# One transposing DMA per group of blocks for O and per two pairs for k in a windowed-attention and MLP kernel

## The chip, the cores and the metric

The kernel runs on one core of a Trainium2 chip. Its engines are TensorE (PE: matmuls, and PEld: the loads of their stationary operand), VectorE (DVE), ScalarE (ACT), GpSimd (POOL) and SyncE (SP). The metric is device time of one execution in microseconds (us), lower is better. A profile describes one execution; its span runs from the first to the last instruction.

## The reference

Eight batches of eight heads, 576 tokens, head size 64. Attention looks back 64 tokens; its output goes through a two-layer MLP with SiLU between.

```python
scores = scale * np.matmul(q, k.transpose(0, 1, 3, 2))
rel = pos[:, None] - pos[None, :]
mask = (rel >= 0) & (rel < window)            # window = 64
...
attn = np.exp(scores)
attn = attn / (np.sum(attn, axis=-1, keepdims=True) + 1e-09)
out = np.matmul(attn, v)
...
x = attn_out.transpose(0, 2, 1, 3).reshape(B * S, H * D)    # 4608 x 512
h = x @ w_in                                                # 512 x 2048
g = h * (1.0 / (1.0 + np.exp(-h)))
return g @ w_out                                            # 2048 x 512
```

## The kernel before

**Tiling.** The heads of a batch form four pairs (NP), and its 576 tokens nine blocks of 64, taken in three groups (NG) of three blocks. A unit of attention is one pair in one group, so a batch has twelve units, in the order of groups and in each group of pairs. The MLP runs over nine tiles of 512 tokens: sixteen first-layer rows of four accumulating matmuls each (L403), a SiLU on ScalarE into a buffer g (L409), then four second-layer rows of sixteen matmuls (L412), a copy into ot (L418) and a store (L422).

**One unit.** TensorE makes the scores of three blocks from kt and qbd (L317) into a bank of PSUM, ScalarE takes exp (L335), VectorE multiplies with the mask (L338), TensorE multiplies with V (L343), VectorE takes the reciprocal of the row sums (L349) and normalizes. The first layer needs the result with features on the partitions, in the tile bridge.

**Two ways to transpose.** In batches 0 to 2 the result O is turned by TensorE (L383, L394) and copied to bridge (L399). From batch 3 on (NXO) the norm writes rows into ox (L367; two units share one tile, in the upper and the lower half of its partitions), and SyncE issues a transposing DMA per unit, from 64 x 384 to three 128 x 64 pieces of bridge (L388). k of batches 0 and 1 is loaded, cast and turned by TensorE (L282, lifted by L295). From batch 2 on (NXK) GpSimd loads k with a casting DMA per head into kb (L240), and SyncE issues a transposing DMA per pair, from 96 x 768 into kt (L246). q is always loaded in float32 (L228, from batch 3 on by SyncE), cast (L271), turned by TensorE (L282) and lifted into qbd (L289). V goes by GpSimd's DMA (L252). kt, qbd and vv have two buffers each, for even and odd batches.

**Order.** Every engine has its instructions in a fixed order, which a planner (class Plan) works out when the kernel is built. It simulates the engines with given durations. Work is added in classes; each class is a queue of its own, taken strictly in the order of adding, and an engine that comes free takes the head with the lowest rank among the classes whose head has all that it needs. Both kinds of transposes stand in the class "xbar" (L457 and L526, rank -1.5), reckoned with 0.5 us of SyncE each, and 1.45 us (k) or 0.55 us (O) of DMA. The work of a batch is added as: q and k, V, the MLP tiles that have become possible, then attention. GpSimd's loads all stand in the class "dma". q and k of a batch are held back until V of the batch before has landed (L456, L470). Scores are planned only at certain points of the MLP (scores_may_run). At run time each instruction waits for the real events of what it needs, so an instruction that the planner put too early blocks what stands behind it on its engine. This holds for SyncE's queue as well, which has all q loads from batch 3 on, all transposes and all stores.

**Buffers.** kb has four tiles, one for a pair (a batch in all); ox six tiles with twelve units in batches 3 to 7, and one unit per tile in batch 0; g has NFT + 4 = 20 tiles. bridge is four tiles, one for each 128 features, of all 4608 tokens.

Of the kernel before, what the change touches and what calls it, by code (L numbers as in the profile page):

```python
# [9 lines left out]
BF16 = mybir.dt.bfloat16  # L10
# [98 lines left out]
def kernel(ctx, tc, q, k, v, w_in, w_out, out):  # L109
    nc = tc.nc  # L110
    B, H, S, D = q.shape
    d_model, d_ff = w_in.shape
    assert (B, H, S, D) == (8, 8, 576, 64) and (d_model, d_ff) == (512, 2048)
    NP = H // 2
    NB = S // 64
    NM = 6
    NR = S // NM
    NG = 3
    NDC = d_model // 128
    NFT = d_ff // 128  # L120
    TT = 512
    NTT = B * S // TT
    TB = TT // 64
    NK = 2
    NN, NNB, NE, NOB, NOT, NGT = 8, 8, 14, 6, 4, NFT + 4
    PARTS = {0: [(0, 192), (192, 384), (384, TT)], 1: [(0, 256), (256, TT)]}
    NXK, NXO = 2, 3
    NKB, NOX = 4, 6
    scale = 1.0 / float(D) ** 0.5


# [2 lines left out]
    keep = ctx.enter_context(tc.tile_pool(name="keep", bufs=1))  # L134
# [11 lines left out]
    kt = [keep.tile([128, 64 + NP * S], BF16, name=f"kt{i}") for i in range(NK)]  # L146
    vv = [keep.tile([128, H * NB + 1, D + 2], BF16, name=f"vv{i}") for i in range(NK)]
    es = [keep.tile([128, 3, 2, 64], BF16, name=f"e{i}") for i in range(NE)]
    rcs = [keep.tile([128, 3, 2], FP32, name=f"rc{i}") for i in range(4)]
    obs = [keep.tile([128, 3, 128], BF16, name=f"ob{i}") for i in range(NOB)]  # L150
    kbs = [keep.tile([NR, NM, 128], BF16, name=f"kb{i}") for i in range(NKB)]
    oxs = [keep.tile([128, 3, 128], BF16, name=f"ox{i}") for i in range(NOX)]
    gts = [keep.tile([128, TT], BF16, name=f"g{i}") for i in range(NGT)]
    ots = [keep.tile([128, d_model], FP32, name=f"ot{i}") for i in range(NOT)]
    bridge = [keep.tile([128, B * S], BF16, name=f"bridge{c}") for c in range(NDC)]
    w_in_sb = keep.tile([128, NDC, d_ff], BF16, name="w_in_sb")
    w_out_sb = keep.tile([128, NFT, d_model], BF16, name="w_out_sb")
    banks = [psum.tile([128, 512], FP32, name=f"at{i}") for i in range(4)]
# [1 line left out]

    p = Plan(
        {"at": range(4), "mp": range(4, 8), "all": range(8)},
        rank=dict(one=-9, dma=-1, ld0=-1, ld1=-1, st=-2, xbar=-1.5, silu=-3, out=-2, pv=0, ot=0, s=1, moe=99, warm=200, turn=2,
                  norm=0, inverse=0, bridge=0, exp=1, mask=1, lift=2, shift=2, cast=4, late=5, clear=9),
        rank0=dict(cast=-6, lift=-5, shift=-4.5, exp=-4, mask=-4, inverse=-3.5, norm=-3, bridge=-3.2),
    )
# [71 lines left out]

    def load_k_rows(w, b, pj, hh):
        nc.gpsimd.dma_start(  # L240
            out=kbs[w][:, :, 64 * hh:64 * hh + 64],
            in_=k[b, 2 * pj + hh].rearrange("(m p) d -> p m d", p=NR),
        )

    def turn_k(w, b, pj):
        nc.sync.dma_start_transpose(  # L246
            out=kt[b % NK][:, 64 + pj * S:64 + (pj + 1) * S].rearrange("x (m p) -> x m p", m=NM),
            in_=kbs[w].rearrange("p m x -> p (m x)"))

    def load_v(e, b, part):  # L250
        g0, g1 = part * 9, part * 9 + 9
# [59 lines left out]
    def at_pv(op):  # L311
        return banks[op["bank"]][:, 0:6 * (D + 1)].rearrange("k (x h y) -> k x h y", x=3, h=2)
# [46 lines left out]
            nc.scalar.mul(ob[r, x, r], pv[r, x, hh, 0:D], rc[r, x, hh:hh + 1])  # L359

    def ox(n):
        return oxs[n // 2 % NOX][64 * (n % 2):64 * (n % 2) + 64]

    def normal_rows(op, n, hh):
        pv, rc = at_pv(op), rcs[n % 4]
# [2 lines left out]

    def normal_both(e, op, n):

        pv, rc, ob = at_pv(op), rcs[n % 4], oxs[n % NOX]
        if e == "DVE":
            nc.vector.tensor_mul(ob.rearrange("k x (h d) -> k x h d", h=2), pv[:, :, :, 0:D],
                                 rc.unsqueeze(3).to_broadcast([128, 3, 2, D]))
            return
        for x in range(3):
            nc.scalar.mul(ob[:, x].rearrange("k (h d) -> k h d", h=2), pv[:, x, :, 0:D], rc[:, x, 0:1])

    def back_both(op, n):
        for x in range(3):  # L380
            for hh in range(2):
                r = slice(64 * hh, 64 * hh + 64)
                nc.tensor.matmul(banks[op["bank"]][r, 64 * x:64 * x + 64], lhsT=oxs[n % NOX][:, x, r],  # L383
                                 rhs=ident[:, r], start=(x == 0), stop=(x == 2))

    def turn_o(n, b, pj, g):
        c0 = b * S + g * 192
        nc.sync.dma_start_transpose(  # L388
            out=bridge[pj][:, c0:c0 + 192].rearrange("x (t i) -> x t i", t=3),
            in_=ox(n).rearrange("i t x -> i (t x)"))  # L390

    def back(op, n):
        for x in range(3):
# [1 line left out]
                             rhs=twoi, start=(x == 0), stop=(x == 2))  # L395

    def to_bridge(e, op, b, pj, g):
        c0 = b * S + g * 192
        copies[e](out=bridge[pj][:, c0:c0 + 192], in_=banks[op["bank"]][:, 0:192])  # L399


    def first_layer(bank, j, ft, c, lo, hi):
        nc.tensor.matmul(  # L403
            banks[bank["bank"]][:, lo:hi], lhsT=w_in_sb[:, c, ft * 128:(ft + 1) * 128],
            rhs=bridge[c][:, j * TT + lo:j * TT + hi], start=(c == 0), stop=(c == NDC - 1),
        )

    def silu(bank, gt, lo, hi):
# [17 lines left out]
    v_landed = {}  # L426
    kq_done, v_done, s_last, pv_last = {}, {}, {}, {}
    nat_free, natb_free = {}, {}
    g_pv, g_norm, g_back, o_done = [], [], [], []
    moe = []  # L430
    exps = {}
# [13 lines left out]

    def add_batch_qk(b):
        pool = "at" if b else "all"
        for pj in range(NP):
            kq_done[(b, pj)] = []
            busy = s_last.get((b - NK, pj), []) + ([c_k[b % NK]] if b < NK else [])  # L450
            for kk in range(2):
                if b >= NXK and kk:
                    w = n_kb[0] % NKB
                    n_kb[0] += 1
                    ca = [p.add("dma", {"POOL": 0.72}, lambda _, w=w, pj=pj, hh=hh: load_k_rows(w, b, pj, hh),
                                [kb_free.get(w)] + (v_landed[b - 1] if b > 2 else []), dma=0.6) for hh in range(2)]  # L456
                    kb_free[w] = p.add("xbar", {"SP": 0.5}, lambda _, w=w, pj=pj: turn_k(w, b, pj), ca + busy, dma=1.45)  # L457
                    kq_done[(b, pj)].append(kb_free[w])
                    continue
                w = n_nat[1] % NNB  # L460
                n_nat[1] += 1
                if b == 0 and kk and pj >= 2:
                    ca = [p.add("dma", {"POOL": 0.72}, lambda _, w=w, pj=pj, hh=hh: load_k_cast(w, b, pj, hh),
                                [natb_free.get(w)], dma=0.6) for hh in range(2)]
                else:
                    i = n_nat[0] % NN
                    n_nat[0] += 1
                    cls, us = ("dma", {"POOL": 0.85}) if b in (1, 2) else ("ld0", {"SP": 0.45})
                    ld = p.add(cls, us, lambda e, i=i, pj=pj, kk=kk: load_qk(e, i, b, pj, kk),
                               [nat_free.get(i)] + (v_landed[b - 1] if b > 2 else []), dma=1.1)  # L470
                    ca = [p.add("cast", {"ACT": 0.84, "DVE": 0.56}, lambda e, i=i, w=w: cast(e, i, w),
                                [ld, natb_free.get(w)], b=b)]
                    nat_free[i] = ca[0]
                tu = p.add("turn", {"PE": 0.27}, None, ca + [c_ident] + busy, lat=0.1, pool=pool, b=b)
                tu["fn"] = lambda _, tu=tu, w=w: turn(tu, w)
                natb_free[w] = tu
                by = {"ACT": 0.64, "DVE": 0.75}
                if kk:
                    li = [p.add("lift", by, lambda e, tu=tu, pj=pj: lift_k(e, tu, b, pj), [tu] + busy, b=b)]
                else:  # L480
# [14 lines left out]
                v_done[(b, pj)] = sh + [lv[pj]]  # L495

    def add_batch_attention(b):
        pv_last[b] = []
        pool = "at" if b else "all"
        for g, pj in [(g, pj) for g in range(NG) for pj in range(NP)]:  # L500
                n = len(g_pv)
# [150 lines left out]
```

## Time and profile before

| | |
|---|---|
| median of three runs | 340.9 us (340.54 to 341.39) |
| profiled execution, its own time | 338.97 us |
| span of the profiled execution | 337.3 us |
| mean granted clock of TensorE | 0.988 |
| DMA queues, share of 16 engines' span | GpSimd's 58.9%, SyncE's 27.9% |
| SyncE waiting at O transposes for norms (DVE ox) | 21.5 us in 23 waits |
| SyncE waiting at k transposes for k rows | 55.9 us in 6 waits |

How such a profile is read: the page lists busy time per engine, the span in 40 slices, the chain of work that ended last, and the costliest groups of instructions, each as line, engine, operation, output<-input, shapes, count, then busy us and mean ns, then the idle time before them with what ended it. "SPq" is the queue of SyncE, in which issuing a DMA takes time though no engine computes. A matmul's duration contains its way through the array, so 382 ns for 512 columns doesn't mean that the next one starts 382 ns later. The timeline lists instructions in order of time as start, duration, engine, line, operation and count, and in brackets the idle time before and what ended it. The chain of waits follows the work that ended last back from the end. Times in all views are counted from the start of the span.

### The profile page before, as it was taken

Reading aid. Unit: us, or ns where it says so; the run is one execution under the profiler, and the core shown is the slowest. Engines: PE = TensorE matmul, PEld = TensorE weight load, DVE = VectorE, ACT = ScalarE, POOL = GpSimd, SP = SyncE. Lnnn points to the kernel's source line nnn. Section 1 sums busy time; section 2 is a strip of 40 time slices with the busy share of each in tenths; the row PEclk is TensorE's granted clock in tenths of the full one; section 3 lists DMA queues with packets and bytes.
Section 4 is the critical chain, followed back from the end, with each engine's and each line's share of the span. In section 5 each row is a group of like instructions: output and inputs, shape, how many; then the busy total and the mean of one; then the engine's idle time right before and its main releaser. Section 6 shows DMA issues by size and latency. Waiting matters only on the chain.

```text
span 337.3 us, 6480 instructions
## 1 busy us (share of the span) xinstructions
PE 316.2 (94%) x2349; PEld 179.6 (53%) x2349; DVE 176.5 (52%) x487; ACT 207.1 (61%) x415; POOL 96.2 (29%) x126
## 2 busy tenths in 40 slices
PE   3989999999999995997998999999999999999994
PEld 1768776588655552653554446545544444444441
DVE  7895978876789880785387808821970000000000
ACT  4679786898888982655842975278437316425611
POOL 8948858572431003800640065000000000000000
PEclk9999999999999997997999999999999999999999
DMA  8999999999999316996997599241231010011011
GB/s 201 164 192 272 175 224 181 137 292 122 217 132 181 85 37 90 160 152 177 105 137 180 126 100 142 65 117 37 58 97 45 31 62 33 0 68 60 0 62 62
DMA packets 114175, 40.30 MB, mean 119 GB/s; under 512 B 97632, under 2 KB 108768, under 8 KB 114144
## 3 DMA queue, kind: packets, MB, share of 16 engines
q0 software_dynamic: 75520, 16.29, 58.9%
q1 hardware_dynamic: 38624, 23.61, 27.9%
q8 instruction: 18, 0.29, 0.4%
q14 instruction: 13, 0.11, 0.1%
HBM read 36.70 MB, written 9.44 MB: 137 GB/s over the span
## 4 chain that ended last, share of the span: by engine, by line
PE 84%; DVE 7%; DMA 4%; issue 2%; ACT 1%; SPq 1%; ACTq 0%; DVEq 0%
PE mp L412 35%; PE mp L403 34%; PE at L343 4%; PE at L317 4%; PE at L282 3%; DVE qbd L289 2%; DMA kt<-kb 2%; DMA nat<-in_q_dram 2%; SPq L388 1%; PE at L594 1%; DVE natb L271 1%; DVE vv L303 1%; DVE ox L367 1%; PE at L394 1%; DVE qbd L211 1%
## 5 line engine op out<-in xcount | busy, mean ns | idle before, releaser
L412 PE MATMUL mp<-w_out_sb,g 128*128 128x512 bf16 x576 | 148.8, 382 | 0.0
L403 PE MATMUL mp<-bridge,w_in_sb 128*128 128x512 bf16 (+3 forms) x768 | 134.3, 328 | 1.1 <-ACT g L409 1.0
L409 ACT ACTIVATE g<-mp 128x512 bf16<-128x512 f32 (+3 forms) x192 | 89.8, 491 | 25.1 <-PE mp L403 23.8
L403 PEld LDWEIGHTS <-w_in_sb 128*128 128x128 bf16 x768 | 69.4, 98 | 52.0 <-issue 2.6
L412 PEld LDWEIGHTS <-g 128*128 128x128 bf16 x576 | 53.1, 98 | 43.4 <-issue 1.4
L240 POOL DMA_DIRECT2D kb<-in_k_dram x48 | 34.9, 733 | 90.1 <-DMA kt<-kb 87.0
L418 ACT COPY ot<-mp 128x512 f32<-128x512 f32 x27 | 15.8, 585 | 62.3 <-PE mp L412 55.9
L338 DVE TENSOR_TENSOR e<-e,mask 128x384 bf16<-128x384 bf16 x84 | 26.0, 350 | 40.3 <-ACT e L335 39.6
L335 ACT ACTIVATE e<-at 128x384 bf16<-128x384 f32 x88 | 38.2, 495 | 14.5 <-PE at L317 13.9
L367 DVE TENSOR_TENSOR ox<-at,rc 64x192 bf16<-64x192 f32 x120 | 42.4, 353 | 2.7
L252 POOL DMA_DIRECT2D vv<-in_v_dram x32 | 32.7, 1034 | 10.5 <-DVE rc L349 7.4
L343 PE MATMUL at<-vv,e 128*128 128x130 bf16 x276 | 30.9, 219 | 0.9 <-DVE vv L303 0.5
L343 PEld LDWEIGHTS <-e 128*128 128x128 bf16 x288 | 23.0, 96 | 15.9 <-DVE e L338 3.0
L289 DVE COPY qbd<-at 64x576 bf16<-64x576 bf16 x35 | 26.0, 753 | 8.3 <-PE at L282 7.0
L317 PE MATMUL at<-qbd,kt 128*128 128x128 bf16 x252 | 23.7, 220 | 4.1 <-DMA kt<-kb 4.1
L282 PE MATMUL at<-ident,natb 96*128 96x96 bf16 x228 | 16.6, 214 | 10.5 <-ACT natb L271 9.5
L317 PEld LDWEIGHTS <-kt 128*128 128x128 bf16 x252 | 18.0, 98 | 13.3 <-DMA kt<-kb 5.4
L282 PEld LDWEIGHTS <-natb 96*128 96x128 bf16 x240 | 14.5, 104 | 18.4 <-ACT natb L271 11.1
L349 DVE RECIPROCAL rc<-at 128x6 f32<-128x6 f32 x92 | 17.6, 194 | 11.8 <-PE at L343 9.2
L271 ACT CAST natb<-nat 96x768 bf16<-96x768 f32 x21 | 17.1, 827 | 8.4 <-DMA nat<-in_q_dram 8.2
L289 ACT COPY qbd<-at 64x576 bf16<-64x576 bf16 x27 | 16.9, 632 | 6.2 <-DVE qbd L289 5.4
L355 DVE TENSOR_TENSOR ob<-at,rc 64x192 bf16<-64x192 f32 x48 | 16.8, 350 | 0.9
(67 smaller groups left out, 162.2 us busy)
## 6 DMA issues: line engine op xcount, KB each, us to landing
out_dram<-ot SPq DMA_DIRECT2D x36, 256.0 KB, 2.3
nat<-in_q_dram SPq DMA_DIRECT2D x24, 288.0 KB, 4.9
vv<-in_v_dram POOLq DMA_DIRECT2D x32, 144.0 KB, 5.5
kb<-in_k_dram POOLq DMA_DIRECT2D x48, 72.0 KB, 5.3
nat<-in_q_dram POOLq DMA_DIRECT2D x8, 288.0 KB, 9.3
w_in_sb<-in_moe_w_in_dram POOLq DMA_DIRECT2D x8, 256.0 KB, 8.5
w_out_sb<-in_moe_w_out_dram POOLq DMA_DIRECT2D x8, 256.0 KB, 8.0
nat<-in_k_dram POOLq DMA_DIRECT2D x4, 288.0 KB, 9.3
```

What stands on the lines that cost most here:

```text
L240: nc.gpsimd.dma_start(out=kbs[w][:, :, 64 * hh:64 * hh + 64], in_=k[b, 2 * pj + hh].rearrange("(m p) d -> p m d", p=NR),)
L252: queue[e].dma_start(out=vv[b % NK][:, 2 * g0 + 1:2 * g1 + 1:2, 0:D], in_=v[b].rearrange("h s d -> (h s) d").rearrange("(g p) d -> p g d", ...
L282: nc.tensor.matmul(pst[:, m], lhsT=natbs[w][:, m], rhs=ident[0:NR, 0:NR], is_transpose=True, start=(m == 0), stop=(m == NM - 1),)
L289: copies[e](out=qbd[b % NK][r, pj, hh].rearrange("x (p m) -> x p m", m=NM), in_=at_bf16(op)[r].rearrange("x (m p) -> x p m", m=NM),)
L317: nc.tensor.matmul(at_sp(op)[:, x], lhsT=kt[b % NK][:, pj * S + t * 64:pj * S + t * 64 + 128], rhs=qbd[b % NK][:, pj, :, t * 64:t * 64 + 6 ...
L335: nc.scalar.activation(out=es[n % NE], in_=at_sp(op), func=ACTF.Exp, scale=scale)
L338: nc.vector.tensor_mul(es[n % NE], es[n % NE], mask0 if g == 0 else mask)
L343: nc.tensor.matmul(at_pv(op)[:, x], lhsT=es[n % NE][:, x].rearrange("p h i -> p (h i)"), rhs=vv[b % NK][:, s:s + NB + 1:NB, 0:D + 1], star ...
L367: nc.vector.tensor_mul(ox(n)[:, :, r], pv[r, :, hh, 0:D], rc[r, :, hh:hh + 1].to_broadcast([64, 3, 64]))
L403: nc.tensor.matmul(banks[bank["bank"]][:, lo:hi], lhsT=w_in_sb[:, c, ft * 128:(ft + 1) * 128], rhs=bridge[c][:, j * TT + lo:j * TT + hi], ...
L409: nc.scalar.activation(out=gts[gt][:, lo:hi], in_=banks[bank["bank"]][:, lo:hi], func=ACTF.Silu)
L412: nc.tensor.matmul(banks[bank["bank"]], lhsT=gts[gt][:, m * 128:(m + 1) * 128], rhs=w_out_sb[:, f, :], start=(f == 0), stop=(f == NFT - 1),)
```

## The change

O of all four pairs of a group is collected in one tile (ox now [128, 3, 4, 128], two groups to a tile, two tiles), and one transposing DMA per group moves 64 x 1536 into bridge. Two pairs of k share one kb tile (two tiles), and one DMA per two pairs moves 96 x 1536 into kt. bridge becomes one tile [128, 72, 4, 64]: token block, then feature chunk, then the 64 tokens, so that such a DMA writes one contiguous stretch; the copies of batches 0 to 2 and the first layer's moving operand follow that layout. The class "xbar" is split into "xo" (rank -1.5) and "xk" (rank -1.4), each reckoned with 1.4 us of SyncE and 2.0 or 2.9 us of DMA. g has one tile less.

```diff
-    NN, NNB, NE, NOB, NOT, NGT = 8, 8, 14, 6, 4, NFT + 4
+    NN, NNB, NE, NOB, NOT, NGT = 8, 8, 14, 6, 4, NFT + 3
...
-    NKB, NOX = 4, 6
+    NKB, NOX = 2, 2
...
-    kbs = [keep.tile([NR, NM, 128], BF16, name=f"kb{i}") for i in range(NKB)]
-    oxs = [keep.tile([128, 3, 128], BF16, name=f"ox{i}") for i in range(NOX)]
+    kbs = [keep.tile([NR, 2, NM, 128], BF16, name=f"kb{i}") for i in range(NKB)]
+    oxs = [keep.tile([128, 3, NP, 128], BF16, name=f"ox{i}") for i in range(NOX)]
...
-    bridge = [keep.tile([128, B * S], BF16, name=f"bridge{c}") for c in range(NDC)]
+    bridge = keep.tile([128, B * NB, NDC, 64], BF16, name="bridge")
...
-        rank=dict(... xbar=-1.5, ...
+        rank=dict(... xo=-1.5, xk=-1.4, ...
...
-            out=kbs[w][:, :, 64 * hh:64 * hh + 64],
+            out=kbs[w][:, pj % 2, :, 64 * hh:64 * hh + 64],
...
-    def turn_k(w, b, pj):
+    def turn_k(w, b, pp):
         nc.sync.dma_start_transpose(
-            out=kt[b % NK][:, 64 + pj * S:64 + (pj + 1) * S].rearrange("x (m p) -> x m p", m=NM),
-            in_=kbs[w].rearrange("p m x -> p (m x)"))
+            out=kt[b % NK][:, 64 + 2 * pp * S:64 + 2 * (pp + 1) * S].rearrange("x (m p) -> x m p", m=2 * NM),
+            in_=kbs[w].rearrange("p j m x -> p (j m x)"))
...
     def ox(n):
-        return oxs[n // 2 % NOX][64 * (n % 2):64 * (n % 2) + 64]
+
+        i, pj = divmod(n, NP)
+        return oxs[i // 2 % NOX][64 * (i % 2):64 * (i % 2) + 64, :, pj]
+
+    def ox0(n):
+        return oxs[n // NP % NOX][:, :, n % NP]
...
-    def turn_o(n, b, pj, g):
-        c0 = b * S + g * 192
+    def turn_o(n, b, g):
+        n0, i = b * NB + 3 * g, n // NP
         nc.sync.dma_start_transpose(
-            out=bridge[pj][:, c0:c0 + 192].rearrange("x (t i) -> x t i", t=3),
-            in_=ox(n).rearrange("i t x -> i (t x)"))
+            out=bridge[:, n0:n0 + 3].rearrange("x t j i -> x (t j) i"),
+            in_=oxs[i // 2 % NOX][64 * (i % 2):64 * (i % 2) + 64].rearrange("i t j x -> i (t j x)"))
...
-        c0 = b * S + g * 192
-        copies[e](out=bridge[pj][:, c0:c0 + 192], in_=banks[op["bank"]][:, 0:192])
+        n0 = b * NB + 3 * g
+        copies[e](out=bridge[:, n0:n0 + 3, pj], in_=banks[op["bank"]][:, 0:192].rearrange("x (t i) -> x t i", t=3))
...
-            rhs=bridge[c][:, j * TT + lo:j * TT + hi], start=(c == 0), stop=(c == NDC - 1),
+            rhs=bridge[:, (j * TT + lo) // 64:(j * TT + hi) // 64, c], start=(c == 0), stop=(c == NDC - 1),
...
-                    w = n_kb[0] % NKB
+                    w = n_kb[0] // 2 % NKB
                     n_kb[0] += 1
-                    ca = [p.add("dma", {"POOL": 0.72}, lambda _, w=w, pj=pj, hh=hh: load_k_rows(w, b, pj, hh),
-                                [kb_free.get(w)] + (v_landed[b - 1] if b > 2 else []), dma=0.6) for hh in range(2)]
-                    kb_free[w] = p.add("xbar", {"SP": 0.5}, lambda _, w=w, pj=pj: turn_k(w, b, pj), ca + busy, dma=1.45)
-                    kq_done[(b, pj)].append(kb_free[w])
+                    k_rows += [p.add("dma", {"POOL": 0.72}, lambda _, w=w, pj=pj, hh=hh: load_k_rows(w, b, pj, hh),
+                                     kb_free.get(w, []) + (v_landed[b - 1] if b > 2 else []), dma=0.6) for hh in range(2)]
+                    k_busy += busy
+                    if pj % 2:
+                        xk = p.add("xk", {"SP": 1.4}, lambda _, w=w, pj=pj: turn_k(w, b, pj // 2), k_rows + k_busy, dma=2.9)
+                        kb_free[w] = [xk]
+                        for i in (pj - 1, pj):
+                            kq_done[(b, i)].append(xk)
+                        k_rows, k_busy = [], []
...
                     no = [p.add("norm", by, lambda e, pv=pv, n=n, hh=hh: normal_rows(pv, n, hh),
-                                [rc] + g_back[n - 2 * NOX:n - 2 * NOX + 1], b=b) for hh in range(2)]
+                                [rc] + xo.get(n // NP - 2 * NOX, []), b=b) for hh in range(2)]
...
-                    xo = p.add("xbar", {"SP": 0.5}, lambda _, n=n, pj=pj, g=g: turn_o(n, b, pj, g), no, dma=0.55)
-                    g_back.append(xo)
-                    o_done.append(xo)
+                    o_rows += no
+                    if pj == NP - 1:
+                        xo[n // NP] = [p.add("xo", {"SP": 1.4}, lambda _, n=n, g=g: turn_o(n, b, g), o_rows, dma=2.0)]
+                        o_done.extend(xo[n // NP] * NP)
+                        o_rows = []
+                    g_back.append(None)
...
                     no = [p.add("norm", {"DVE": 0.56, "ACT": 0.9}, lambda e, pv=pv, n=n: normal_both(e, pv, n),
-                                [rc] + g_back[n - NOX:n - NOX + 1] * (n >= NOX))] * 2
+                                [rc] + g_back[n - NP * NOX:n - NP * NOX + 1] * (n >= NP * NOX))] * 2
```

More of the change, by code (lines that the diff above doesn't have):

```diff
@@ L162 @@
         {"at": range(4), "mp": range(4, 8), "all": range(8)},
-        rank=dict(one=-9, dma=-1, ld0=-1, ld1=-1, st=-2, xbar=-1.5, silu=-3, out=-2, pv=0, ot=0, s=1, moe=99, warm=200, turn=2,
+        rank=dict(one=-9, dma=-1, ld0=-1, ld1=-1, st=-2, xo=-1.5, xk=-1.4, silu=-3, out=-2, pv=0, ot=0, s=1, moe=99, warm=200, turn=2,
                   norm=0, inverse=0, bridge=0, exp=1, mask=1, lift=2, shift=2, cast=4, late=5, clear=9),
@@ L369, in normal_both @@
     def normal_both(e, op, n):
-        pv, rc, ob = at_pv(op), rcs[n % 4], oxs[n % NOX]
+        pv, rc, ob = at_pv(op), rcs[n % 4], ox0(n)
         if e == "DVE":
@@ L382, in back_both @@
                 r = slice(64 * hh, 64 * hh + 64)
-                nc.tensor.matmul(banks[op["bank"]][r, 64 * x:64 * x + 64], lhsT=oxs[n % NOX][:, x, r],
+                nc.tensor.matmul(banks[op["bank"]][r, 64 * x:64 * x + 64], lhsT=ox0(n)[:, x, r],
                                  rhs=ident[:, r], start=(x == 0), stop=(x == 2))
-    def turn_o(n, b, pj, g):
-        c0 = b * S + g * 192
+    def turn_o(n, b, g):
+        n0, i = b * NB + 3 * g, n // NP
         nc.sync.dma_start_transpose(
-            out=bridge[pj][:, c0:c0 + 192].rearrange("x (t i) -> x t i", t=3),
-            in_=ox(n).rearrange("i t x -> i (t x)"))
+            out=bridge[:, n0:n0 + 3].rearrange("x t j i -> x (t j) i"),
+            in_=oxs[i // 2 % NOX][64 * (i % 2):64 * (i % 2) + 64].rearrange("i t j x -> i (t j x)"))
     def back(op, n):
@@ L428 @@
     nat_free, natb_free = {}, {}
+    xo = {}
     g_pv, g_norm, g_back, o_done = [], [], [], []
@@ L452, in add_batch_qk @@
                 if b >= NXK and kk:
-                    w = n_kb[0] % NKB
+                    w = n_kb[0] // 2 % NKB
                     n_kb[0] += 1
-                    ca = [p.add("dma", {"POOL": 0.72}, lambda _, w=w, pj=pj, hh=hh: load_k_rows(w, b, pj, hh),
-                                [kb_free.get(w)] + (v_landed[b - 1] if b > 2 else []), dma=0.6) for hh in range(2)]
-                    kb_free[w] = p.add("xbar", {"SP": 0.5}, lambda _, w=w, pj=pj: turn_k(w, b, pj), ca + busy, dma=1.45)
-                    kq_done[(b, pj)].append(kb_free[w])
+                    k_rows += [p.add("dma", {"POOL": 0.72}, lambda _, w=w, pj=pj, hh=hh: load_k_rows(w, b, pj, hh),
[6 more added lines that the diff above has]
+                            kq_done[(b, i)].append(xk)
+                        k_rows, k_busy = [], []
                     continue
@@ L497, in add_batch_attention @@
     def add_batch_attention(b):
-        pv_last[b] = []
+        pv_last[b], o_rows = [], []
         pool = "at" if b else "all"
```

## The prediction, made before the changed kernel ran

> **What bounds the kernel now.** I read the page first: TensorE is busy for nearly the whole span, and from 254 us on, after the last attention work, only two-layer matmuls follow, back to back. So only time in which TensorE idles, or runs at a lower clock, can be won.
>
> ```profile
> span 337.3 us, 6480 instructions
> PE 316.2 (94%) x2349; PEld 179.6 (53%) x2349; DVE 176.5 (52%) x487; ACT 207.1 (61%) x415; POOL 96.2 (29%) x126
> ```
>
> The second view is busy time by stretch. Behind the start-up I looked for stretches whose PE time is below their length or whose clock is below 1. Columns: stretch, length, busy time and count of PE, PEld, DVE, ACT, POOL, then clock, DMA share, GB/s.
>
> ```profile
> 36.00:106.00 70.00, 68.28 (x731) 48.98 (x728) 57.49 (x152) 56.98 (x139) 37.91 (x48) 1.00 1.72 180
> 122.00:136.00 14.00, 10.09 (x54) 4.71 (x53) 4.83 (x10) 6.71 (x12) 4.07 (x6) 0.88 0.53 79
> 136.00:152.00 16.00, 16.00 (x119) 9.00 (x118) 14.15 (x47) 9.92 (x19) 5.69 (x7) 1.00 1.53 153
> 152.00:160.00 8.00, 5.70 (x29) 2.71 (x28) 4.02 (x6) 4.19 (x8) 0.00 (x0) 0.79 0.71 186
> 181.00:186.00 5.00, 3.38 (x32) 1.81 (x31) 2.93 (x10) 2.33 (x4) 0.00 (x0) 1.00 0.93 241
> 186.00:260.00 74.00, 73.99 (x459) 37.92 (x457) 37.65 (x111) 46.07 (x81) 9.79 (x12) 1.00 0.54 88
> ```
>
> Three holes stand out: 14.00 - 10.09 = 3.91 us, 8.00 - 5.70 = 2.30 us and 5.00 - 3.38 = 1.62 us. In the first two stretches the granted clock also fell: 14 x (1 - 0.88) = 1.68 us and 8 x (1 - 0.79) = 1.68 us of matmul time were lost. The calm stretches beside them lose nothing. From 36 to 106 us another 1.72 us is idle, in small pieces.
>
> The third view is the timeline of TensorE, for what ended each hole. The fourth is the chain of waits in order of time around them.
>
> ```profile
> 130.95 0.34 PE L317 MATMUL at<-qbd,kt 128*128 128x128 bf16 x3 [3.91 <-DMA kt<-kb]
> 155.35 0.64 PE L282 MATMUL at<-ident,natb 96*128 96x96 bf16 x6 [2.30 <-ACT natb L271]
> 184.35 0.43 PE L282 MATMUL at<-ident,natb 96*128 96x96 bf16 x6 [1.62 <-ACT natb L271]
> ```
>
> ```profile
> 128.58 2.33 DMA kt<-kb
> ...
> 150.34 0.66 SPq L388
> 151.06 3.38 DMA nat<-in_q_dram
> ...
> 179.72 0.42 SPq L388
> 180.19 3.25 DMA nat<-in_q_dram
> ```
>
> The first hole waits for k of batch 4 to be transposed; the other two wait for a q load, its cast, and then the turn. All three go back to a DMA that SyncE issued late, directly behind O transposes. The timeline of SyncE's queue shows why.
>
> ```profile
> 111.60 16.81 SPq L388 DMA_TRANSPOSE bridge<-ox  x12
> 128.58 5.27 SPq L246 DMA_TRANSPOSE kt<-kb  x4
> ```
>
> Twelve O transposes of batch 3 hold SyncE for 16.81 us, 1.40 us each, where the planner reckons 0.5 us (L526). The four k transposes of batch 4 start only behind the last of them.
>
> **The change, part by part.** *Fewer, larger transposes.* The rows of the two source lines give the issue time (min/median/max, ns) and the time to landing.
>
> ```profile
> L388 SPq DMA_TRANSPOSE bridge<-ox x60: 1163/1186/2164, 111.6 to 254.1; - x60
> ...
> DMA to landing us min/median/max: 2.3/2.4/6.9
> ```
>
> ```profile
> L246 SPq DMA_TRANSPOSE kt<-kb x24: 1196/1196/3212, 52.6 to 228.7; - x24
> ...
> DMA to landing us min/median/max: 2.3/3.7/11.7
> ```
>
> An O transpose moves 64 x 384 bf16, 49 KB; a k transpose 96 x 768, 147 KB: three times the bytes for 10 ns more issue time and the same shortest landing. So I take issue time as independent of size. The 60 + 24 issues hold SyncE 60 x 1.186 + 24 x 1.196 = 99.9 us; the 15 + 12 new ones would hold it 15 x 1.186 + 12 x 1.196 = 32.1 us. The other end: time by bytes, four times for O (4.74 us) and twice for k (2.39 us), which is 99.9 us again. I take the constant, which the rows of two sizes support. The new planner costs, 1.4 us each, then lie above the hardware, not below it as now.
>
> By the Trainium skill (DMA: Bandwidth & Descriptors, "Why a DMA increments its semaphore by 16 and not by 1", table of issue costs) earlier generations push one command per transposed tile, so issue would grow with size; that speaks against this part. Here 49 KB and 147 KB differ by 10 ns, so the trace doesn't bear it out between these sizes, and by that rule the sum would be that of the second rival.
>
> *k and O ordered apart.* Today both stand in one class of the planner, taken in order of adding; k of batch 4 is added behind all of O of batch 3 and must follow it. With classes of their own, k of batch 4 needs only its rows and the scores of batch 2. The rows were there long before, as GpSimd's timeline shows:
>
> ```profile
> 88.31 1.45 POOL L240 DMA_DIRECT2D kb<-in_k_dram  x2 [0.57 <-DMA kt<-kb]
> ...
> 131.49 2.91 POOL L240 DMA_DIRECT2D kb<-in_k_dram  x4 [27.23 <-DMA kt<-kb]
> 138.75 3.97 POOL L252 DMA_DIRECT2D vv<-in_v_dram  x4
> ```
>
> The last rows of batch 4 were issued at 88 to 90 us; with even the longest landing of a transpose, 11.7 us, added for each of the load and the transpose, kt of batch 4 would stand at about 113 us, against a need at 127.0 us (130.95 - 3.91). Hole one goes: 3.91 + 1.68 = 5.59 us. What is late next there? The scores also need a bank, held by the lifts of batch 5:
>
> ```profile
> 122.24 2.99 ACT L289 COPY qbd<-at 64x576 bf16<-64x576 bf16 x5
> 124.19 2.11 DVE L289 COPY qbd<-at 64x576 bf16<-64x576 bf16 x3 [0.38 <-ACT qbd L289]
> ```
>
> These end at 125.23 and 126.30 us, before 127.0.
>
> The early k transposes also free kb early. GpSimd waited 27.23 us for that; its k rows of batch 5, V of batch 5 behind them, and then the q loads of batch 6, which the planner lets go only when V of batch 5 has landed, all move forward. V of batch 5 then waits for the last PV matmuls of batch 3 instead:
>
> ```profile
> 119.06 0.33 PE L343 MATMUL at<-vv,e 128*128 128x130 bf16 x3
> ```
>
> The moved loads are eight k rows and four V on GpSimd, four q on SyncE. The stretch they move into has room, GpSimd idle and few DMAs under way (share 0.46 against 1.72 from 36 to 106 us):
>
> ```profile
> 106.00:122.00 16.00, 16.00 (x116) 8.68 (x115) 14.11 (x45) 14.09 (x24) 0.00 (x0) 1.00 0.46 116
> ```
>
> So V of batch 5 is issued near 120 instead of 138.75, and q of batch 6 some 19 us earlier, near 132 instead of 151.06: ahead of most O transposes of batch 4, and far ahead of its need. Hole two goes: 2.30 + 1.68 = 3.98 us. The same chain one batch later moves q of batch 7 (180.19): hole three, 1.62 us.
>
> *What is added.* An O transpose now waits for all four pairs of its group (L526), a k transpose for four k loads. Queued behind one on SyncE are stores, q loads and the next transposes. The first layer reads bridge long after: nowhere on the page does TensorE wait for bridge<-ox. Later landing of O is therefore taken at nothing; should that cover go, a group's last row lands at most 4 x 2.4 - 2.4 = 7.2 us later. The k pairs are late at most in batches 2 and 3, where rows arrive just in time; price 0 to the third rival's, taken at nothing. The O buffers hold 16 units instead of 12 (8 instead of 6 in batch 0), so no norm waits longer for one.
>
> One g buffer fewer touches ScalarE's silu. The row of its waits (total us, times, longest):
>
> ```profile
> ACT g L409 <- PE mp L403: 23.8, 84, 0.8
> ```
>
> It waits only for the first layer, never for the second layer to free a g, so I take nothing; at most each of seven tiles would lose one longest wait of 0.8 us, 5.6 us.
>
> *The bridge by token block.* The first layer's moving operand becomes runs of 64 columns instead of one, and its copies write such runs. Rows with and without runs, mean ns after the busy time:
>
> ```profile
> L317 PE MATMUL at<-qbd,kt 128*128 128x128 bf16 x252 | 23.7, 220 | 4.1 <-DMA kt<-kb 4.1
> L403 PE MATMUL mp<-bridge,w_in_sb 128*128 128x128 bf16 x64 | 4.1, 219 | 0.4 <-ACT g L409 0.4
> L367 DVE TENSOR_TENSOR ox<-at,rc 64x192 bf16<-64x192 f32 x120 | 42.4, 353 | 2.7
> L399 DVE CAST bridge<-at 128x192 bf16<-128x192 f32 x14 | 5.0, 355 | 1.5 <-PE at L394 0.6 <-PE at L383 0.5
> ```
>
> L317 reads two runs of 64, L403 one of 128: 220 against 219 ns. L367 writes three runs, L399 one: 353 against 355 ns. I take nothing. The upper end is 1 ns for each of seven more runs in 448 full matmuls of the first layer, 3.1 us; the lower end is nothing, since one run is already at the same rate.
>
> **The sum.** 3.91 + 2.30 + 1.62 + 1.68 + 1.68 = 11.19 us. For a reordered plan I give back 0.5 us of small waits (an estimate: under a third of the 1.72 us that 36 to 106 us shows). Profiled execution: 338.97 - 10.7 = 328.3 us, against a span of 337.3 and 1.7 us around it. The median of the runs is 340.9, 1.9 us above the profiled one; the same gain gives **330.2 us**. No loss at all and all of the 1.72 us won as well would be 328.0; the three runs reach 0.4 us below their median, so the low end is 327.6.
>
> **Rivals.**
> *One hole stays or a new one opens* (0.15). TensorE works in a fixed order, so one operand late is enough: the q loads could again stand behind a waiting O transpose. For it: two of three holes were that. Against it: the chain that releases them moves by some 19 us. Price: one hole with its clock loss, 2.30 + 1.68 to 5.59 us, so about 334 to 336. The two holes that drew a clock loss were 3.91 and 2.30 us, the one that didn't 1.62. The Trainium skill (TensorE: Matmul & The Clock Gate, "Part 1: The HAM clock gate") asks an idle window of about 3.4 us for the lower clock; by that a 2.3 us hole alone would cost no clock, but the trace shows it did, and the measurement decides.
> *The issue grows with size* (0.05): the change doesn't relieve SyncE, 99.9 us as before. k apart from O still closes hole one, but q stands behind 4.74 us transposes: 3.98 + 1.62 us stay, about 335.3 us.
> *Slower* (0.05): k of batch 3. In that stage the DMAs are crowded:
>
> ```profile
> L246 SPq DMA_TRANSPOSE kt<-kb x4: 1201/1255/3212, 71.2 to 80.7; - x4
> ...
> DMA to landing us min/median/max: 7.1/10.5/11.7
> ```
>
> ```profile
> 92.58 0.33 PE L317 MATMUL at<-qbd,kt 128*128 128x128 bf16 x3
> ```
>
> Its last transpose goes out at 80.7 us and lands 7.1 us later, near 87.8; its scores follow at 92.58. A pair that waits for four loads can use up these 4.8 us, and TensorE then stops. Each further us costs one, with 1.68 us of clock once. It decides beyond 4.8 + 11.2 - 1.7 = 14.3 us of lateness; at 18 us the kernel takes about 344.6 us. Against it: the pair waits for two loads more, 1.45 us of issue.
> *No change* (0.03): two holes with their clock loss come back elsewhere, 2 x 5.59 = 11.2 us, and the time stays at 340.9.
>
> **How the numbers follow.** Forecast 0.72, rivals 0.15, 0.05, 0.05, 0.03. The range is 327.6 to 336: it takes in the forecast's own 327.6 to 332, the first two rivals (up to 335.3, and 0.5 for the forecast's small waits), and leaves out no change, slower and part of the forecast's edges. About 0.3% is what a measurement of this kernel tells from no change; below 339.9 us lie 0.72 + 0.15 + 0.05 = 0.92; the same 0.03; slower 0.05.
>
> **What would show it.** Right: 15 O and 12 k transposes at about 1.2 us on SyncE; k of batch 4 issued before O of batch 3; no wait of GpSimd for kt<-kb near 27 us; q of batch 6 issued well before 150 us; no stretch behind 106 us with PE below its length, clock 1.00. Wrong: transposes of 2.4 or 4.7 us; PE holes ended by kt<-kb or natb at new places, above all near 92 us; first-layer matmuls longer than 382 ns on average in this form:
>
> ```profile
> L403 PE MATMUL mp<-bridge,w_in_sb 128*128 128x512 bf16 x448 | 102.4, 382 | 0.0
> ```

## The result, and the profile after

The changed kernel takes 326.87 us in the median (326.77 to 327.37), the kernel before 340.72 us; the ratio is 0.962, 95% interval 0.9545 to 0.9695. The forecast was 330.2 us; the median lies 0.7 us below the low end of its range, 327.6. The profiled execution takes 326.77 us against 338.97, 12.2 us less, where the forecast took off 10.7. Here and below, ratios leave out runs over 1.5% above the fastest of the same kernel; medians count all.

The page of the changed kernel (span, then busy time of each engine):

```profile
span 324.7 us, 6343 instructions
PE 311.7 (96%) x2349; PEld 179.0 (55%) x2349; DVE 172.0 (53%) x480; ACT 207.8 (64%) x420; POOL 96.8 (30%) x126
```

Busy time by stretch, for the same stretches as before; the columns are length, PE, PEld, DVE, ACT, POOL, clock, DMA share, GB/s:

```profile
0.00:36.00 36.00, 29.26 (x346) 22.18 (x347) 27.55 (x72) 25.90 (x63) 29.02 (x43) 1.00 1.39 204
36.00:106.00 70.00, 67.79 (x704) 47.85 (x702) 56.24 (x146) 54.50 (x134) 38.90 (x50) 1.00 1.75 192
122.00:136.00 14.00, 14.00 (x139) 9.10 (x138) 12.47 (x42) 9.72 (x23) 6.98 (x9) 1.00 1.16 145
152.00:160.00 8.00, 7.97 (x63) 4.42 (x62) 6.04 (x12) 7.34 (x14) 3.29 (x5) 1.00 1.33 223
181.00:186.00 5.00, 5.00 (x39) 2.87 (x38) 4.55 (x16) 3.91 (x8) 0.00 (x0) 1.00 0.10 25
186.00:260.00 74.00, 74.00 (x406) 36.01 (x405) 21.87 (x69) 36.32 (x63) 0.00 (x0) 1.00 0.15 47
```

Where 3.91, 2.30 and 1.62 us of TensorE were idle, it is now idle 0.00, 0.03 and 0.00, and the clock stays at 1.00. The stages shift in time, so the whole from 106 to 186 us counts too: there TensorE is busy 79.97 of 80 us, where it was busy 72.01. From 36 to 106 us it is idle 2.21 us instead of 1.72, 0.5 us more.

SyncE's timeline of the changed kernel, and its issue rows by source line (ns, min/median/max):

```profile
95.00 3.06 SPq L246 DMA_TRANSPOSE kt<-kb  x2
...
104.47 1.98 SPq L228 DMA_DIRECT2D nat<-in_q_dram  x4
113.23 1.22 SPq L393 DMA_TRANSPOSE bridge<-ox  x1
...
140.75 1.94 SPq L228 DMA_DIRECT2D nat<-in_q_dram  x4
```

```profile
L393 SPq DMA_TRANSPOSE bridge<-ox x15: 1217/1222/1408, 113.2 to 211.5; - x15
...
DMA to landing us min/median/max: 2.9/3.5/7.4
```

```profile
L246 SPq DMA_TRANSPOSE kt<-kb x12: 1247/1340/2758, 54.9 to 167.6; - x12
```

k of batch 4 is issued at 95.0 us, ahead of all O of batch 3, instead of 128.6. An O transpose of four times the bytes takes 1.222 us to issue against 1.186. The q loads of batch 6 go out at 140.75 instead of 151.06. GpSimd's timeline shows the loads between:

```profile
105.19 6.33 POOL L240 DMA_DIRECT2D kb<-in_k_dram  x8
127.27 2.97 POOL L252 DMA_DIRECT2D vv<-in_v_dram  x3 [15.76 <-DVE e L338]
131.99 0.99 POOL L252 DMA_DIRECT2D vv<-in_v_dram  x1 [1.75 <-PE at L343]
```

All of this reads as the forecast's mechanism. The experiments show that it is not what was needed.

### The profile page after: what moved, and what is told of

It reads as the page before. It is cut to its first block, busy times and chain, and to the rows that moved or that the text cites. A ratio compares the mean times of both kernels' runs of the same rounds, so it can differ in the third digit from the quotient of the medians.

```text
span 324.7 us, 6343 instructions
## 1 busy us (share of the span) xinstructions
PE 311.7 (96%) x2349; PEld 179.0 (55%) x2349; DVE 172.0 (53%) x480; ACT 207.8 (64%) x420; POOL 96.8 (30%) x126
## 4 chain that ended last, share of the span: by engine, by line
PE 88%; DVE 9%; issue 1%; ACT 0%; ACTq 0%
PE mp L417 38%; PE mp L408 35%; PE at L343 5%; PE at L317 4%; DVE qbd L289 3%; PE at L282 2%; DVE natb L271 1%; DVE vv L303 1%; DVE vv L305 1%; PE at L609 1%; PE at L399 1%; DVE qbd L211 1%; PE at L388 0%; DVE kt L295 0%; DVE ob L214 0%
## 5 line engine op out<-in xcount | busy, mean ns | idle before, releaser
L417 PE MATMUL mp<-w_out_sb,g 128*128 128x512 bf16 x576 | 146.9, 379 | 0.0
L423 ACT COPY ot<-mp 128x512 f32<-128x512 f32 x24 | 14.0, 585 | 55.1 <-PE mp L417 55.0
L240 POOL DMA_DIRECT2D kb<-in_k_dram x48 | 35.8, 756 | 25.8 <-DMA kt<-kb 23.2
L343 PEld LDWEIGHTS <-e 128*128 128x128 bf16 x288 | 22.7, 96 | 16.1 <-DVE e L338 2.5
L343 PE MATMUL at<-vv,e 128*128 128x130 bf16 x276 | 30.1, 219 | 0.8 <-DVE vv L303 0.5
L338 DVE TENSOR_TENSOR e<-e,mask 128x384 bf16<-128x384 bf16 x84 | 25.8, 349 | 8.3 <-ACT e L335 7.7
L289 DVE COPY qbd<-at 64x576 bf16<-64x576 bf16 x29 | 21.8, 753 | 8.0 <-PE at L282 3.4
L289 ACT COPY qbd<-at 64x576 bf16<-64x576 bf16 x33 | 20.8, 630 | 6.6 <-DVE qbd L289 4.1
L271 ACT CAST natb<-nat 96x768 bf16<-96x768 f32 x20 | 16.2, 834 | 3.3 <-DMA nat<-in_q_dram 3.1
```

The lines of the kernel that those rows point to most:

```text
L240: nc.gpsimd.dma_start(out=kbs[w][:, pj % 2, :, 64 * hh:64 * hh + 64], in_=k[b, 2 * pj + hh].rearrange("(m p) d -> p m d", p=NR),)
L289: copies[e](out=qbd[b % NK][r, pj, hh].rearrange("x (p m) -> x p m", m=NM), in_=at_bf16(op)[r].rearrange("x (m p) -> x p m", m=NM),)
L338: nc.vector.tensor_mul(es[n % NE], es[n % NE], mask0 if g == 0 else mask)
L343: nc.tensor.matmul(at_pv(op)[:, x], lhsT=es[n % NE][:, x].rearrange("p h i -> p (h i)"), rhs=vv[b % NK][:, s:s + NB + 1:NB, 0:D + 1], star ...
L417: nc.tensor.matmul(banks[bank["bank"]], lhsT=gts[gt][:, m * 128:(m + 1) * 128], rhs=w_out_sb[:, f, :], start=(f == 0), stop=(f == NFT - 1),)
```

## The experiments

Three theories were set against each other. *Order*: the holes come from k standing behind O in one class. *Issue time*: SyncE is held too long by 84 issues. *Cost*: the planner reckons 0.5 us for what takes 1.4 us, and so puts instructions where their operands aren't there yet. A fourth, *fewer issues*, came in later: the error does harm in proportion to the transposes that stand behind each other. In the table each ratio is to runs of the kernel before that were taken beside that row, with medians of 340.4 to 341.9 us, so medians of rows that differ by about 1 us are not told apart.

| kernel | order | cost 1.4 | merged | median us | ratio to before, 95% interval |
|---|---|---|---|---|---|
| classes apart | yes | no | no | 340.07 | 0.999 (0.9944 to 1.0038) |
| cost 0.95 | no | half | no | 337.88 | 0.9915 (0.988 to 0.995) |
| cost | no | yes | no | 331.61 | 0.976 (0.9655 to 0.9861) |
| apart, cost | yes | yes | no | 328.45 | 0.9665 (0.9594 to 0.9735) |
| apart, cost, layout | yes | yes | no | 327.74 | 0.962 (0.9603 to 0.9636) |
| merged | no | no | both | 327.39 | 0.961 (0.9579 to 0.9636) |
| merged, apart | yes | no | both | 327.85 | 0.964 (0.9604 to 0.9684) |
| merged, cost | no | yes | both | 326.94 | 0.961 (0.9535 to 0.9684) |
| O merged | no | no | O | 326.88 | 0.958 (0.9559 to 0.9608) |
| k merged | no | no | k | 329.52 | 0.967 (0.9627 to 0.9715) |
| the change | yes | yes | both | 326.87 | 0.962 (0.9545 to 0.9695) |

**Classes apart, nothing else.**

```diff
-        rank=dict(... xbar=-1.5, ...
+        rank=dict(... xo=-1.5, xk=-1.4, ...
-                    kb_free[w] = p.add("xbar", {"SP": 0.5}, ...
+                    kb_free[w] = p.add("xk", {"SP": 0.5}, ...
-                    xo = p.add("xbar", {"SP": 0.5}, ...
+                    xo = p.add("xo", {"SP": 0.5}, ...
```

> The kernel before with k and O in classes of their own (ranks -1.4 and -1.5); still 60 + 24 transposes, still reckoned with 0.5 us each. Theory 'order' (the holes come from k of a batch standing behind all O of the batch before, and from the chain of loads behind that): k of batch 4 goes out near 95 to 105 us instead of 128.6, all three holes go, 328 to 330 us. Theory 'issue time' (twelve O transposes of 1.4 us hold SyncE too long in each batch): hole one goes, but q loads still come late behind O, 333 to 337 us. Theory 'cost' (the planner's 0.5 us for what takes 1.4 us puts instructions too early): holes of 2 to 5 us at other places, 333 to 341 us.

340.07 us, no change that can be measured. SyncE's timeline of this run, the timelines of ScalarE and of TensorE, and its busy time by stretch:

```profile
92.16 3.19 SPq L246 DMA_TRANSPOSE kt<-kb  x2
...
134.24 2.48 SPq L388 DMA_TRANSPOSE bridge<-ox  x2
136.81 0.53 SPq L422 DMA_DIRECT2D out_dram<-ot  x1
137.43 3.79 SPq L388 DMA_TRANSPOSE bridge<-ox  x3
141.27 1.55 SPq L228 DMA_DIRECT2D nat<-in_q_dram  x3
```

```profile
147.17 0.83 ACT L271 CAST natb<-nat 96x768 bf16<-96x768 f32 x1 [9.12 <-DMA nat<-in_q_dram]
148.02 0.87 ACT L335 ACTIVATE e<-at 128x384 bf16<-128x384 f32 x2
...
148.57 1.12 PE L317 MATMUL at<-qbd,kt 128*128 128x128 bf16 x9 [8.70 <-ACT e L335]
```

```profile
136.00:152.00 16.00, 7.25 (x47) 4.24 (x48) 5.32 (x17) 6.62 (x13) 3.43 (x4) 0.79 1.51 170
```

k of batch 4 is as early as in the changed kernel, 92.2 us, and the hole that waited for it is gone. But the planner now sees q of batch 6 early and puts its cast ahead of exps on ScalarE. On the chip that load stands behind a run of O transposes of 1.2 us each, goes out at 141.27 and lands some 6 us later. The cast holds ScalarE for 9.12 us, the exps behind it hold the banks, and TensorE waits 8.70 us. One hole took the place of another. The forecast's step fails here, in the way of its first rival.

**The planner's cost, nothing else.**

```diff
-                    kb_free[w] = p.add("xbar", {"SP": 0.5}, ...
+                    kb_free[w] = p.add("xbar", {"SP": 1.4}, ...
-                    xo = p.add("xbar", {"SP": 0.5}, ...
+                    xo = p.add("xbar", {"SP": 1.4}, ...
```

> The kernel before with the planner's SyncE time of a transpose set from 0.5 to 1.4 us and nothing else; one class, 60 + 24 transposes. Theory 'cost': the planner puts other matmuls where TensorE now waits, the holes go, 328 to 331 us. Theory 'order': k of batch 4 still leaves behind all O of batch 3, near 128 us; the planner knows it and may fill part of it, 333 to 340 us. Theory 'issue time': SyncE stays the limit of each batch, 335 to 341 us.

331.61 us, 0.6 us above the range of *cost* and below the 333 us and more of the two others. Two numbers that the chip never sees take off 9 us, by the order of instructions that comes of them. SyncE's timeline and that of TensorE:

```profile
126.63 5.17 SPq L388 DMA_TRANSPOSE bridge<-ox  x3
...
136.46 2.57 SPq L246 DMA_TRANSPOSE kt<-kb  x2
```

```profile
150.52 0.83 PE L317 MATMUL at<-qbd,kt 128*128 128x128 bf16 x12
```

k of batch 4 leaves even later than before, 136.5 us. But TensorE's order has the scores of batch 4 at 150.5, one phase of the MLP later, 14 us behind the issue of k. In the kernel before TensorE was ready for them at 127.0 us (130.95 - 3.91), 1.5 us before k was even issued (128.58). Part of what is missing to the changed kernel's time is idle time elsewhere: 2.73 us from 186 to 260 us, of which 1.87 us go back to q loads that were issued at 180.50 us, behind k transposes. Both *order* and *issue time* fall as the necessary cause: k still follows all O, and SyncE issues the same 84 transposes.

**Both planner edits**: the two diffs above together.

> Both edits at once (classes of their own, 1.4 us reckoned), still 60 + 24 transposes of 1.2 us. Theories 'order' and 'cost': no hole behind 106 us, 327 to 330 us, the larger transposes are then not needed for the gain. Theory 'issue time': SyncE is still held 99.9 us by transposes, at least one hole stays, 332 us or more.

328.45 us: most of the gain, with 84 issues.

**Merged, back in one class.**

```diff
-        rank=dict(... xo=-1.5, xk=-1.4, ...
+        rank=dict(... xbar=-1.5, ...
```

> The changed kernel with k and O back in one class (rank -1.5, strictly in the order of adding); 15 + 12 transposes, reckoned 1.4 us. Theory 'order': k of batch 4 leaves behind the last O of batch 3, which needs all norms of batch 3, so k comes near 125 to 133 us and a hole of some us comes back, 330 to 336 us. Theories 'issue time' and 'cost': as the changed kernel, 326 to 328 us.

326.94 us, the same as the change. SyncE's timeline and TensorE's:

```profile
132.01 1.22 SPq L393 DMA_TRANSPOSE bridge<-ox  x1
133.41 0.45 SPq L427 DMA_DIRECT2D out_dram<-ot  x1
134.08 2.80 SPq L246 DMA_TRANSPOSE kt<-kb  x2
```

```profile
149.86 0.83 PE L317 MATMUL at<-qbd,kt 128*128 128x128 bf16 x12
```

k comes at 134.1, a microsecond behind the 125 to 133 us that *order* had named, and no hole follows: the scores stand at 149.9. *Order* is settled as neither needed nor enough.

**Merged, with the old cost.** The two 1.4 of the changed kernel become 0.5.

> The changed kernel with its transposes reckoned at 0.5 us of SyncE again instead of 1.4; 15 + 12 transposes and classes of their own stay. Theory 'cost' in its strict form (what matters is that the planner's number is true): holes come back, 333 us or more. Theory 'fewer issues' (a wrong number does harm only in proportion to the count of transposes that stand behind each other: 0.9 us times three O and two k of a batch is under 5 us, against 0.9 times sixteen = 14 us before): at most one small hole, 327 to 330 us.

327.85 us. A wrong number is nearly harmless once few transposes carry it.

**Cost halfway.** As the run of the cost alone, with 0.95 in place of 1.4.

> The kernel before with its transposes reckoned at 0.95 us, halfway between 0.5 (before) and 1.4 (the run that changed the cost alone, 331.6 us). Theory 'cost': the holes shrink with the error that is left, 332 to 338 us. If the time jumps at a point (one hole or none), it lies at either end, 331 to 332 or 340 to 342 us.

337.88 us, 333.29 to 340.51 over nine runs. The profiled execution is the fastest of the nine (333.29 us). In it there are still three holes:

```profile
122.00:136.00 14.00, 11.84 (x59) 5.47 (x58) 5.78 (x13) 5.62 (x9) 4.35 (x6) 0.88 0.59 89
136.00:152.00 16.00, 14.99 (x98) 7.87 (x99) 10.30 (x32) 10.23 (x18) 5.40 (x6) 1.00 1.60 142
152.00:160.00 8.00, 6.29 (x46) 3.24 (x46) 2.66 (x5) 5.56 (x10) 0.00 (x0) 1.00 0.53 146
```

2.16 us with the clock at 0.88, 1.01 us and 1.71 us, 4.88 us in all where the kernel before had 7.83. The median lies in the 332 to 338 us of *cost*, and not in the 331 to 332 or 340 to 342 us of a jump, which fits holes that shrink with the error that is left. How large they are in a run of median time was not seen.

**O from batch 2** (NXO 3 to 2) and **k from batch 1** (NXK 2 to 1), each in the changed kernel, to win more now that transposes are cheap for SyncE.

```diff
-    NXK, NXO = 2, 3
+    NXK, NXO = 2, 2
```

> The changed kernel with O of batch 2 going by transposing DMAs too (NXO 3 to 2): TensorE loses 36 matmuls of line 399 (29 ns apart, 1.0 us), ScalarE and VectorE 12 copies to bridge, SyncE gets 3 transposes of 1.2 us in the crowded stage. If TensorE bounds there, 325.5 to 326 us; if the crowded DMAs make O or what stands behind it late, 327 to 332 us.

```diff
-    NXK, NXO = 2, 3
+    NXK, NXO = 1, 3
```

> The changed kernel with k of batch 1 by row loads and transposes too (NXK 2 to 1): TensorE loses 24 turns of line 282 (42 ns apart, 1.0 us), VectorE and ScalarE 4 casts and 4 lifts, GpSimd gets 8 loads for 4 in the stage where its DMAs are busiest. If TensorE bounds, 325.5 to 326 us; if k of batch 1 lands late, 328 to 336 us.

327.95 and 327.48 us: neither beats 326.87. The microsecond that TensorE saves comes back as idle time. From 36 to 106 us it is busy 67.33 of 70 us with O and 67.29 with k, instead of 67.79; from 106 to 186 it is busy 78.17 and 77.53 of 80 us instead of 79.97:

```profile
106.00:186.00 80.00, 78.17 (x595) 44.47 (x602) 66.08 (x202) 65.10 (x114) 27.48 (x34) 1.00 1.45 177
```

```profile
106.00:186.00 80.00, 77.53 (x608) 44.57 (x615) 65.23 (x193) 65.36 (x119) 27.50 (x33) 1.00 1.43 172
```

**Only the larger transposes.** The changed kernel with one class and 0.5 us: neither of the planner's edits.

> The changed kernel without its two edits of the planner: one class in the order of adding, 0.5 us reckoned; only the larger transposes, the layout and one g less remain. Theory 'fewer issues' (harm = error of the reckoning times transposes that stand behind each other; order is worth nothing): 326.5 to 329 us. Theory 'cost or order needed': one hole or more comes back, 331 us or more.

327.39 us: merging carries the gain without either edit. One thing goes with it: the larger transposes are also reckoned with longer DMA times (2.0 us in place of 0.55 for O, 2.9 in place of 1.45 for k), in every merged run of the table. No run has the merging without them, so what they add isn't known.

**Only O merged**, and **only k merged**, each with one class and 0.5 us.

> As the run before, but only O in large transposes (15), k still one DMA per pair (24, four kb tiles). Theory 'fewer issues': the twelve O of a batch were what piled up, so nearly all of the gain stays, 326.5 to 330 us. If k's four per batch matter as much, 332 us or more.

326.88 us, as *fewer issues* says. Timelines of VectorE (the last norms of batch 3), of SyncE and of TensorE, in the profiled execution (330.80 us, the longest of the four):

```profile
123.88 2.24 DVE L372 TENSOR_TENSOR ox<-at,rc 64x192 bf16<-64x192 f32 x6
127.53 5.31 SPq L246 DMA_TRANSPOSE kt<-kb  x4
132.25 0.33 PE L317 MATMUL at<-qbd,kt 128*128 128x128 bf16 x3
```

k of batch 4 leaves 1.4 us after the last norm (126.12 to 127.53), and the scores find it there. In the kernel before it left 6.3 us after it (122.26 to 128.58):

```profile
120.02 2.24 DVE L367 TENSOR_TENSOR ox<-at,rc 64x192 bf16<-64x192 f32 x6
```

> The kernel before with only k in large transposes (12 for 24), O still one per unit (60), old layout, one class, 0.5 us reckoned. Theory 'fewer issues': two issues of 1.2 us less per batch of sixteen, the pile of O stays, 336 to 342 us. If k's late arrival alone made the holes, 328 to 332 us.

329.52 us (327.81 to 331.28), against an expected 336 to 342: a miss. It lies in the 328 to 332 us of the other reading, that k's late arrival alone made the holes, but k doesn't come earlier here. Twelve O per batch still pile up on SyncE. SyncE's timeline, TensorE's, and the one stretch with a hole:

```profile
112.37 13.35 SPq L388 DMA_TRANSPOSE bridge<-ox  x7
...
134.08 2.79 SPq L246 DMA_TRANSPOSE kt<-kb  x2
```

```profile
149.66 0.83 PE L317 MATMUL at<-qbd,kt 128*128 128x128 bf16 x12
```

```profile
152.00:160.00 8.00, 5.97 (x36) 3.13 (x34) 5.57 (x15) 3.53 (x8) 0.00 (x0) 0.79 0.10 25
```

k leaves 5.5 us later than in the kernel before, yet nothing waits for it. The planner moves the scores of batch 4 from 131 to 149.7 us, as with the cost edit; that it does so because two pairs with their longer DMA are ready later in its eyes is argued, not read from its times. So *fewer issues* alone is not the whole: what counts is how late the operand comes, less the room that its reader has in TensorE's order. Merging O shrinks the first; merging k, or a true cost, enlarges the second, in a jump of a phase of the MLP. The hole at 152 us is the old fault on another path. GpSimd's, VectorE's and TensorE's timelines:

```profile
137.73 5.81 POOL L240 DMA_DIRECT2D kb<-in_k_dram  x8 [34.37 <-DMA kt<-kb]
153.19 0.76 DVE L305 COPY vv<-vv 64x2304 bf16<-64x2304 bf16 x1 [23.07 <-DMA vv<-in_v_dram]
155.16 0.35 PE L343 MATMUL at<-vv,e 128*128 128x130 bf16 x3 [2.03 <-DVE e L338]
```

The late k transposes free kb late, so the k rows of batch 5 and V behind them (143.72 to 149.45 us) go out late. A copy of that V (L305) stands in VectorE's order ahead of mask multiplies (L338) and holds them up, and TensorE waits 2.03 us for one of these.

**The layout.** The run with both planner edits, and the token-block bridge and one g less added; each O transpose writes three runs.

```diff
-            out=bridge[pj][:, c0:c0 + 192].rearrange("x (t i) -> x t i", t=3),
+            out=bridge[:, c0 // 64:c0 // 64 + 3, pj],
...
-            rhs=bridge[c][:, j * TT + lo:j * TT + hi], start=(c == 0), stop=(c == NDC - 1),
+            rhs=bridge[:, (j * TT + lo) // 64:(j * TT + hi) // 64, c], start=(c == 0), stop=(c == NDC - 1),
```

> The kernel with classes of their own and 1.4 us reckoned (328.45 us), still 60 + 24 transposes, with the token-block bridge and one g less added; each O transpose then writes three separate runs. If the layout is free, as the rows of the forecast say: 327.5 to 329.5 us. At 1 ns for each further run in the first layer: 3 us more, 331.5 us. If the layout gives the 1.6 us by which the changed kernel is ahead of that run: 326.5 to 327.5 us.

327.74 us against 328.45 without the layout, intervals overlapping: not slower. The first layer's forms in the changed kernel (mean ns behind the busy time), of which the first took 382 ns before, and 379 ns in the run with both planner edits, which has the old layout and no loss of clock:

```profile
L408 PE MATMUL mp<-bridge,w_in_sb 128*128 128x512 bf16 x448 | 101.6, 379 | 0.0
...
L408 PE MATMUL mp<-bridge,w_in_sb 128*128 128x128 bf16 x64 | 4.1, 219 | 0.5 <-ACT g L414 0.5
```

## Why the prediction was right or wrong, point by point

**What can be won: right.** The three holes and the two losses of clock, 11.19 us, are gone to 0.03 us and nothing. That 36 to 106 us lost just the 0.5 us given back (2.21 - 1.72 us) is luck: in the other kernels run here 2.6 to 4.2 us are idle there. That the span fell by 12.6 us and not 10.7 is spread thin: 36.00 - 29.26 = 6.74 us are idle in the start-up instead of 36.00 - 28.93 = 7.07, and TensorE's busy time fell by 316.2 - 311.7 = 4.5 us, of which the clock explains 3.36. The rest of some 1.1 us of busy time I can't assign. The low end of the range lacked this term.

**Issue time independent of size: right, nearly.** 1.222 us for 196 KB against 1.186 for 49 KB (O); 1.340 for 295 KB against 1.196 for 147 KB (k), in the median. With 15 x 1.222 + 12 x 1.340 = 34.4 us SyncE is held as forecast (32.1). The second rival, issue in proportion to size, is not borne out. Of the per-tile cost of the Trainium skill (DMA: Bandwidth & Descriptors, "Why a DMA increments its semaphore by 16 and not by 1") these rows show at most 0.036 us (O) and 0.144 us (k).

**k and O ordered apart, which was to close hole one and by its chain holes two and three: wrong as the cause.** It happened as told in the changed kernel, but alone it is worth nothing (0.999), and without it the change loses nothing (326.94 us). What showed in its place: any of merging O, merging k or reckoning 1.4 us gives back 9 to 14 us, so neither the order of k and O nor the count of issues had to change, and the planner's 0.5 us is the fault that the cost run alone removes. For hole one its working can be read: O piled up on SyncE until k left 6.3 us after the last norm. The plan's own times were not read; 1.40 - 0.5 = 0.9 us for each transpose is the planner's error, and part of the 1.40 us is waiting for norms (the issue alone takes 1.186).

For holes two and three the pile is not the last link. The chain of waits in the kernel before shows norms there:

```profile
149.97 0.37 DVE ox L367
...
179.35 0.37 DVE ox L367
```

The q loads stood in SyncE's order behind O transposes (150.34 and 179.72 us) that waited for these norms, so the last link there is a norm and not SyncE's issuing. How much of these two holes comes down from hole one and how much from the planner's number was not separated. The forecast had the sentence ("the planner reckons 0.5 us", the new costs "lie above the hardware, not below it as now") and gave it no term of its own. The trace also held the warning: the q loads stood behind O transposes, and an earlier plan for q without a faster SyncE only moves the hole, as the first run shows.

**q of batch 6 some 19 us earlier: mis-sized.** It is 10.3 us (151.06 to 140.75). V of batch 5 goes out at 127.27, not near 120, and at 131.99 for its last part. The forecast took the time of batch 3's last PV matmuls from the old order (119.06), but the new plan has another: its last scores of batch 3 stand behind 118 us, where the kernel before had made them by 102 us.

```profile
118.62 0.83 PE L317 MATMUL at<-qbd,kt 128*128 128x128 bf16 x12
```

So V waits longer for that batch to leave its buffer; the rows of GpSimd above end its idle time with a mask multiply (L338) and with a PV matmul (L343). No hole came of it.

**The layout and the g buffer at nothing: right,** by 379 ns with and without the layout in the full form, 219 and 219 in the smallest, and the layout run.

**The rivals.** A new hole in place of the old one came true for the kernel with the classes apart, not for the change. k of batch 3 too late did not happen; no wait of TensorE for kt<-kb is left in the changed kernel, and TensorE's waits for casts of q in batch 3 and before are at most 0.8 us.

## What to carry to other kernels

Where an order is made by a planner, compare its durations with the trace first: an error that is small for one instruction can add up along a queue, and other engines that follow that order pay for it. A hole is how late the operand comes, less the room that the reader has in its order; an edit can close it by either, so two edits that each close it alone don't add up. If the parts of a change are not run one by one, the mechanism that the trace shows at work can be one that wasn't needed.

## What the runs showed of the hardware

Holes well under 4 us cost clock. Idle times of TensorE of 2.03 us (k merged alone), 2.16 (cost halfway), 2.30 and 3.91 us (before) each came with 1.68 us of lost clock in their stretch, that is about 3.4 us at a clock of 0.50; 1.62 (before) and 1.71 us (cost halfway) came with none. The length of one hole is not all that counts: in the profiled execution with O merged alone, two shorter waits close together were followed by the same half clock (in the last line the clock is the third value from the end).

```profile
76.62 0.43 PE L282 MATMUL at<-ident,natb 96*128 96x96 bf16 x6 [0.83 <-ACT natb L271]
78.69 0.48 PE L282 MATMUL at<-ident,natb 96*128 96x96 bf16 x6 [1.09 <-DVE natb L271]
80.00:82.00 2.00, 2.00 (x12) 1.42 (x10) 1.59 (x3) 1.14 (x3) 0.00 (x0) 0.50 1.29 95
```

Times of kernels with holes also scatter: beside the first four experiments the kernel before took 338.1 to 346.5 us in thirteen runs, the changed kernel 326.8 to 327.4 in four.
